# Pooled attention feeding a gated unit: bfloat16 norm broadcasts, a shift that is split before one fp16 transpose, and a lead for the output divisions in a list schedule

## The chip, the cores and the metric

The kernel runs on one core of one Trainium2 chip. The metric is the device time of one execution in microseconds (us); the median of several runs is compared. The core's engines are named as the profile names them: PE is TensorE (PEld is its weight load, which overlaps the multiplying), DVE is VectorE, ACT is ScalarE, POOL is GpSimd and SP is SyncE, which here issues all DMAs.

## What is computed

The reference has two stages. The first is attention for 8 batches of 8 heads, with 1152 keys of 64 elements and queries averaged in pairs to 576; the second is a gated feed-forward unit whose gate mixes the positions of the sequence.

```python
q_pool = q.reshape(B, H, S // 2, 2, D).mean(axis=3)
scores = np.matmul(q_pool, k.transpose(0, 1, 3, 2)) / np.sqrt(D)
scores = scores - np.max(scores, axis=-1, keepdims=True)
attn = np.exp(scores)
attn = attn / (np.sum(attn, axis=-1, keepdims=True) + 1e-09)
x = np.matmul(attn, v)                       # heads side by side: 8 x 576 x 512
h = np.maximum(x @ w_in, 0.0)
u, g = h[..., :512], h[..., 512:]
g_n = (g - mean(g)) / np.sqrt(var(g) + 1e-06)
g_s = np.einsum('ts,bsd->btd', w_spatial, g_n) + b_spatial[None, :, None]
out = (u * g_s) @ w_out
```

Everything is float32 for the caller. Inside, each float32 operand is held as a sum of two 16-bit parts (a head and a rest), and products are made of 16-bit matmuls.

## The kernel before

**Units of attention.** Two heads of one batch make a unit; there are 32 units. Unit i needs, ahead of its own loop, `prep(i)` (the queries and keys scaled and split into fp16 parts), `maxima(i)` (the maximum of the scores of each query, from a cheaper product of the fp16 heads alone) and `shift` (the maxima turned into two extra rows of the matmul operand X, so that the product already comes out shifted). `attention(i)` then makes, for each of the two heads, nine tiles of 128 keys by 512 queries: two matmuls into PSUM (L796, L797), the exponential on ACT (L802, into a buffer `pt`, of which there are 8), and on POOL the subtraction that leaves the rest of the tile as fp16 (L822). The last 64 queries of both heads go through tail tiles (L809, L813, L818). `values(i, k)` multiplies a finished tile with the values: twelve short matmuls (L714, L720, L725) that add up over the nine tiles of a head in one PSUM tile `o`. There is one buffer for `o`. When the ninth tile is in, the sums are divided by the denominators: `inverse` makes `den` (L693 and L694), and L733 writes the quotient `xm`. Only then may the next head's first L714 write `o`; and a `pt` buffer is free again only when its L725 has run.

**The maxima.** For each of 9 blocks of 128 queries, three matmuls of 384 columns (L617, and L608 for the block of tails) go to PSUM tiles `pm` or `pw`, and a DVE reduction (L623, `mt`) takes the maximum of each. After block 5 and after block 9, `shift` runs: it reduces `mt` to `mx` with one column for each block (L635, 128 partitions by 5 or 4 columns), PE transposes `mx` in float32 into a `pm` tile of 5 or 4 partitions by 128 columns (L639), and DVE subtracts and scales it there (L642), casts it to fp16 (L645) and subtracts the cast for the rest (L646). Two DMAs put the two rows into X (L649).

**Norms.** `scales` gets a sum of squares per partition, adds it up over the partitions and broadcasts it with one float32 matmul against a tile of ones (L345), and three small DVE operations (L350, L355, L356) make powers of two of it. It runs once for each unit (`sq`, two columns), and for the values of each batch (`vt`), the gate (`gt`) and the three weights (one column each).

**The gated unit.** Two batches (8 units) at a time, `gated_unit` makes the second stage: products with w_in (L879, L943), the spatial mixing (L984, L985) and w_out (L1027). Its steps are taken between those of the attention of later units. Until the first 8 units are done there is none of this work; in that time the weights are loaded and converted from doubles by large DVE and ACT operations (L384 to L396).

**The order of the work.** The program is first written in the order in which the generators are stepped. Then `Order.pin` puts each engine's instructions into a new order with a list schedule: it goes through modelled time with costs from `cost`, and on each engine takes, of the instructions that are ready at the modelled time, the one that stands first in the program. That order is then fixed with dependencies. A lock is modelled as well: `two_from_sbuf` names DVE operations whose inputs all lie in SBUF, and `pin` lets such an operation and one of POOL not overlap. The engines execute in that order, each instruction waiting for what it depends on.

Of the kernel before, what the change touches and what calls it, by code (L numbers as in the profile page):

```python
# [10 lines left out]
F16 = mybir.dt.float16  # L11
# [20 lines left out]
class Order:  # L32
# [6 lines left out]
    def __init__(self):  # L39
        self.slot = {}  # L40
        self.count = {}
        self.lined = []
        self.seen = 0

# [12 lines left out]
    def line(self, tc, skip=False):  # L57


        n = len(tc.nc.cur_bb.bb.instructions)  # L60
        self.lined.append((self.seen, n, skip))
        self.seen = n

# [119 lines left out]
    def pin(self, tc):  # L183
# [29 lines left out]
        load = {n for n, i in enumerate(prog) if lane[n] == "SP" and i.ins and i.ins[0].bass_ap.tensor.name not in self.slot}  # L213
        last = {}
        dep = mybir.DependencyInfo(mybir.DependencyClass.NoSync, mybir.DependencyReason.DATA)
        for _ in prog:
            best = None
            for e, ns in ready.items():
                if ns:

                    at = {n: max(due[n], wire - 1000) if n in load else due[n] for n in ns}
                    t = max(free[e], min(at.values()))
                    n = min(n for n in ns if at[n] <= t)
                    if best is None or t < best[0]:
                        best = (t, e, n)
# [36 lines left out]
def attn_sgu_kernel(ctx: ExitStack, tc: tile.TileContext, qT, kT, v, w_in, w_spT, b_sp, w_out, out):  # L262
# [41 lines left out]
    ones = const.tile([P, P], F32, name="ones")  # L304
    nc.vector.memset(ones, 1.0)

# [33 lines left out]
    def scales(sq, name, up=0):  # L340
# [4 lines left out]
        nc.tensor.matmul(pt[:, :n], lhsT=ones, rhs=sq, start=True, stop=True)  # L345
# [285 lines left out]
    def shift(st, mt, a, z):  # L631
# [7 lines left out]
        nc.tensor.transpose(out=pt[:n, :P], in_=mx[:, :n], identity=ident)  # L639
        mr = sm.tile([NT, 2, P], F16, name="mr", bufs=2)  # L640
        m = pt[:n, :P]
        nc.vector.tensor_scalar(  # L642
            out=m, in0=m, scalar1=st["lnp"][:n], scalar2=1.0 / MROW, op0=ALU.subtract, op1=ALU.mult
        )
        nc.vector.tensor_copy(out=mr[:n, 0], in_=m)  # L645
        nc.vector.tensor_sub(mr[:n, 1], m, mr[:n, 0])  # L646
        for r in range(2):
            rows = X[D + r : D + r + 1].rearrange("p h s -> p (h s)")
            nc.sync.dma_start(out=rows[:, a * P : z * P], in_=mr[:n, r])  # L649
# [7 lines left out]
    LAG = 2  # L657
    TAIL_SPLIT = 5
# [41 lines left out]
    def values(i, k):  # L700
# [28 lines left out]
        if c == NC - 1:  # L729
            if h == 0:  # L730
                st["xm"] = wk.tile([P, 4, P], F32, name="xm")
            r = inverse(o[:, :, D], "den")
            nc.vector.tensor_tensor(  # L733
                out=st["xm"][:, :, h * D : (h + 1) * D], in0=o[:, :, 0:D],
                in1=r.unsqueeze(2).to_broadcast([P, 4, D]), op=ALU.mult,
            )
# [450 lines left out]
```

## Time and profile before

| | us |
|---|---|
| median of three runs | 1226.53 (1224.41 to 1229.68) |
| span of the profiled execution | 1225.3 |
| PE busy | 1153.0 (94%) |
| DVE busy | 906.2 (74%) |
| ACT busy | 889.2 (73%) |
| POOL busy | 875.8 (71%) |

The profile is of one execution, whose span of 1225.3 us from the first to the last instruction is its own time; the median of the runs is 1.2 us above it. A row of instructions gives the busy time in all, the mean of one in ns, and the idle time of the engine ahead of it with what ended that idle time. A row of the timeline gives the start, the time it took, the engine and line, and in brackets the idle time before it. Matmuls are pipelined: the record of one lasts longer than the time by which it holds up the next, so what a matmul costs PE is read from one start to the next. Consecutive short DVE records overlap as well.

In 40 slices, PE is below 90% busy up to about 280 us and at 90% or more in nearly all slices after that; the granted clock is 0.8 to 0.9 in parts of the first 280 us and full afterwards.

### The profile page before, as it was taken

To read this page: it belongs to the slowest core of one execution; us is meant where nothing else is said; L and a number is where in the kernel's file an instruction comes from. 1 tells how busy PE (TensorE), PEld (TensorE's weight loads), DVE (VectorE), ACT (ScalarE), POOL (GpSimd) and SP (SyncE) were. 2 spreads that over 40 slices of the span, in tenths; PEclk is the share of its full clock that TensorE was granted. 3 is DMA by queue.
4 is the path that set the end of the run, shared out by engine and by line. 5 is a ranking of instruction groups with operands and counts; after the bars stand their busy time and mean duration, and the time that the engine had idled before them with its cause. 6 is when DMAs were issued, how large, how long until landed. Compare 5 with 4: busy or idle time off the path is not lost.

```text
span 1225.3 us, 34090 instructions
## 1 busy us (share of the span) xinstructions
PE 1153.0 (94%) x13632; PEld 725.7 (59%) x13632; DVE 906.2 (74%) x2187; ACT 889.2 (73%) x1659; POOL 875.8 (71%) x750
## 2 busy tenths in 40 slices
PE   3878888889999999999999999999999999999998
PEld 1545566556666666666666666566666666665453
DVE  5699999977889678766679686865669867851644
ACT  4788669778977877868777787878777876754433
POOL 2769979898887877777788877778887776764000
PEclk9899999999999999999999999999999999999999
DMA  5454454446333443155322442146422321111002
GB/s 188 157 180 133 118 180 123 110 115 173 113 89 94 133 126 101 51 145 170 93 75 75 132 134 74 53 133 198 113 75 75 90 84 43 30 45 36 1 1 78
DMA packets 62335, 126.70 MB, mean 103 GB/s; under 512 B 13728, under 2 KB 21920, under 8 KB 61664
## 3 DMA queue, kind: packets, MB, share of 16 engines
q1 hardware_dynamic: 62176, 124.52, 34.7%
q8 instruction: 107, 1.75, 0.6%
q14 instruction: 52, 0.43, 0.1%
HBM read 81.20 MB, written 9.44 MB: 74 GB/s over the span
## 4 chain that ended last, share of the span: by engine, by line
PE 72%; DVE 8%; ACT 2%; POOL 1%; issue 1%; DMA 1%; SPq 1%; ACTq 0%; DVEq 0%; POOLq 0%
PE pss L797 7%; PE pss L796 7%; PE pm L617 7%; PE pw L984 6%; PE pw L879 6%; PE pw L1027 6%; PE pw L943 5%; PE o L725 4%; PE o L714 4%; PE o L720 4%; DVE mt L623 3%; DVE vv L372 2%; PE pss L879 1%; PE pss L984 1%; PE pss L1027 1%
## 5 line engine op out<-in xcount | busy, mean ns | idle before, releaser
L822 POOL TENSOR_TENSOR pt<-pt 128x512 f16<-128x512 f32 x576 | 641.6, 1134 | 185.3 <-ACT pt L802 183.3
L802 ACT ACTIVATE pt<-pss,esc 128x512 f32<-128x512 f32 x576 | 387.7, 687 | 150.0 <-PE pss L797 114.3
L623 DVE TENSOR_REDUCE mt<-pm 128x1 f32<-128x384 f32 x733 | 387.1, 548 | 70.7 <-PE pm L617 61.9
L796 PE MATMUL pss<-qhi,khi 128*128 128x512 f16 x576 | 220.5, 384 | 13.9 <-ACT pt L802 12.8
L797 PE MATMUL pss<-xq,klo 66*128 66x512 f16 x576 | 221.1, 385 | 1.3 <-DMA xq<-mr 1.3
L617 PE MATMUL pm<-khi,qhi 128*128 128x384 f16 x655 | 205.5, 330 | 10.9 <-DVE mt L623 5.9
L714 PEld LDWEIGHTS <-pt 128*128 128x128 bf16 x2304 | 132.2, 99 | 69.1 <-issue 4.7
L725 PE MATMUL o<-vp,pt 128*128 128x65 f16 x2304 | 169.6, 194 | 2.5 <-POOL pt L822 2.4
L714 PE MATMUL o<-vp,pt 128*128 128x65 f16 x2304 | 170.8, 194 | 0.2
L720 PE MATMUL o<-vp,pt 128*128 128x64 f16 x2304 | 168.3, 194 | 0.0
L725 PEld LDWEIGHTS <-pt 128*128 128x128 f16 x2304 | 121.1, 99 | 26.9 <-POOL pt L822 5.0
L617 PEld LDWEIGHTS <-qhi 128*128 128x128 f16 x768 | 73.8, 99 | 81.9 <-issue 38.0
L720 PEld LDWEIGHTS <-pt 128*128 128x128 bf16 x2304 | 112.3, 99 | 3.3 <-issue 0.5
L879 PE MATMUL pw<-wi_h,xg 128*128 128x512 f16 x240 | 88.7, 378 | 0.2 <-DVE mt L623 0.2
L818 ACT ACTIVATE ptl<-pss,esc 128x256 f32<-128x256 f32 (+1 forms) x128 | 63.9, 499 | 27.8 <-PE pss L813 27.0
L822 POOL TENSOR_TENSOR ptl<-ptl 128x1152 f16<-128x1152 f32 x32 | 70.3, 2197 | 18.8 <-ACT ptl L818 18.8
L1027 PE MATMUL pw<-wo_h,vv 128*128 128x512 f16 x216 | 79.7, 379 | 3.9 <-DVE vv L372 3.9
L797 PEld LDWEIGHTS <-klo 66*128 66x128 f16 x576 | 57.1, 99 | 43.3 <-issue 17.4
L984 PE MATMUL pw<-ws_h,vv 128*128 128x512 f16 x216 | 80.6, 379 | 0.0
L943 PE MATMUL pw<-xg,wi_h 128*128 128x512 f16 (+1 forms) x336 | 80.6, 325 | 0.0
L623 DVE TENSOR_REDUCE mt<-pw 128x1 f32<-128x384 f32 x131 | 69.2, 541 | 11.1 <-PE pw L617 10.7
L796 PEld LDWEIGHTS <-khi 128*128 128x128 f16 x576 | 56.7, 99 | 21.0 <-issue 3.6
(194 smaller groups left out, 2446.1 us busy)
## 6 DMA issues: line engine op xcount, KB each, us to landing
vt<-in_v_dram SPq DMA_DIRECT2D x56, 576.0 KB
qt<-in_qT_dram SPq DMA_DIRECT2D x32, 576.0 KB
kt<-in_kT_dram SPq DMA_DIRECT2D x32, 576.0 KB
khi<-kn SPq DMA_DIRECT2D x128, 144.0 KB
out_dram<-row SPq DMA_DIRECT2D x24, 256.0 KB
qhi<-xq SPq DMA_DIRECT2D x64, 72.0 KB
klo<-klo SPq DMA_DIRECT2D x32, 144.0 KB
vv<-in_w_in_dram SPq DMA_DIRECT2D x4, 1024.0 KB
```

The source lines that it names most:

```text
L617: nc.tensor.matmul(pm[:, :W], lhsT=qhl[:, h, c0 : c0 + P], rhs=khh[:, h, n * NB : (n + 1) * NB, :], start=True, stop=True,)
L623: nc.vector.reduce_max(out=mt[:, t, n : n + 1], in_=pm[:, :W], axis=AX.X)
L714: nc.tensor.matmul(o[:, t], lhsT=top[:, cols], rhs=vp[:, D : D + D1], start=c == 0 and t == 0, stop=False, skip_group_check=True,)
L720: nc.tensor.matmul(o[:, t, 0:D], lhsT=top[:, cols], rhs=vp[:, 0:D], start=False, stop=False, skip_group_check=True)
L725: nc.tensor.matmul(o[:, t], lhsT=rst[:, cols], rhs=vp[:, D : D + D1], start=False, stop=c == NC - 1, skip_group_check=True,)
L796: nc.tensor.matmul(o, lhsT=khh[:, h, c, :], rhs=qhl[:, h, q], start=True, stop=False)
L797: nc.tensor.matmul(o, lhsT=KL[0:KR, h, c, :], rhs=X[0:KR, h, q], start=False, stop=True)
L802: nc.scalar.activation(pt, ps, AF.Exp, bias=0.0, scale=esc)
L822: nc.gpsimd.tensor_sub(t.bitcast(F16)[..., 0::2], t, t.bitcast(BF16)[..., 1::2])
L879: nc.tensor.matmul(ph, lhsT=xa[:, cc, c0 : c0 + P], rhs=wa[:, cc, DH:DF], start=n == 0, stop=n == 3 * NCC - 1,)
L984: nc.tensor.matmul(pv, lhsT=l, rhs=r[:, 0:MAIN], **fl)
L1027: nc.tensor.matmul(py, lhsT=ga[:, fc, c0 : c0 + P], rhs=wa[:, fc, :], start=m == 0, stop=m == end - 1)
```

## The change

Three things are changed; the products, tiles and buffers stay.

1. **Norms.** The tile of ones is bfloat16, and the matmul in `scales` takes the upper halves of the float32 sums as bfloat16. The profile before shows two matmul records for each float32 product; a bfloat16 product is one matmul with one weight load.
2. **Shift.** The subtraction, the scaling and the split into two fp16 parts are made on the columns of `mx` in SBUF, 128 partitions by 5 or 4 columns, ahead of the transpose. Both parts stand side by side in `mc` and are transposed by one fp16 transpose into 10 or 8 partitions of a PSUM tile, and one copy brings them to `mr`. The two DMAs are the same.
3. **Lead.** The instructions of the division (the two of `inverse` and the product) are written inside `order.sooner`, which notes a lead of 400 places for each. `pin` chooses among the ready instructions of an engine by place in the program less lead.

```diff
+    def sooner(self, tc, steps, make):
+        ins = tc.nc.cur_bb.bb.instructions
+        n = len(ins)
+        make()
+        for i in tc.nc.cur_bb.bb.instructions[n:]:
+            self.lead[i.name] = steps
...
+        rank = [n - self.lead.get(i.name, 0) for n, i in enumerate(prog)]
...
-                    n = min(n for n in ns if at[n] <= t)
+                    n = min((n for n in ns if at[n] <= t), key=rank.__getitem__)
...
-    ones = const.tile([P, P], F32, name="ones")
+    ones = const.tile([P, P], BF16, name="ones")
     nc.vector.memset(ones, 1.0)
+    ident_h = const.tile([P, P], F16, name="ident_h")
+    nc.vector.tensor_copy(out=ident_h, in_=ident)
...
-        nc.tensor.matmul(pt[:, :n], lhsT=ones, rhs=sq, start=True, stop=True)
+        nc.tensor.matmul(pt[:, :n], lhsT=ones, rhs=sq.bitcast(BF16)[:, 1::2], start=True, stop=True)
...
-        nc.vector.reduce_max(out=mx[:, :n], in_=mt[:, a:z], axis=AX.X)
-        yield
-        yield
-        pt = ps_m.tile([P, 512], F32, name="pm")
-        nc.tensor.transpose(out=pt[:n, :P], in_=mx[:, :n], identity=ident)
-        mr = sm.tile([NT, 2, P], F16, name="mr", bufs=2)
-        m = pt[:n, :P]
-        nc.vector.tensor_scalar(
-            out=m, in0=m, scalar1=st["lnp"][:n], scalar2=1.0 / MROW, op0=ALU.subtract, op1=ALU.mult
-        )
-        nc.vector.tensor_copy(out=mr[:n, 0], in_=m)
-        nc.vector.tensor_sub(mr[:n, 1], m, mr[:n, 0])
+        m = mx[:, :n]
+        nc.vector.reduce_max(out=m, in_=mt[:, a:z], axis=AX.X)
+        nc.vector.tensor_scalar(out=m, in0=m, scalar1=st["lnp"], scalar2=1.0 / MROW, op0=ALU.subtract, op1=ALU.mult)
+        mc = sm.tile([P, 2, NT], F16, name="mc", bufs=2)
+        mh, ml = (mc.rearrange("p r t -> p (r t)")[:, r * n : (r + 1) * n] for r in range(2))
+        nc.vector.tensor_copy(out=mh, in_=m)
+        nc.vector.tensor_sub(ml, m, mh)
+        yield
+        yield
+        pt = ps_m.tile([P, 512], F32, name="pm").bitcast(F16)[: 2 * n, :P]
+        nc.tensor.transpose(out=pt, in_=mc.rearrange("p r t -> p (r t)")[:, : 2 * n], identity=ident_h)
+        mr = sm.tile([2 * NT, P], F16, name="mr", bufs=2)
+        nc.vector.tensor_copy(out=mr[: 2 * n], in_=pt)
...
+    LEAD = 400
...
-            r = inverse(o[:, :, D], "den")
-            nc.vector.tensor_tensor(
+            def divide():
+                r = inverse(o[:, :, D], "den")
+                nc.vector.tensor_tensor(
...
+            order.sooner(tc, LEAD, divide)
```

The order of the instructions moves on every engine. Two places are shown. The first is DVE at the seventh division of the program (the first head of the fourth unit), where the second unit after it is being prepared. Names: `mx` and `mr` belong to the shift, `mt` to the maxima, `qhi` and `klo` to `prep`, `vv` to the conversion of a weight, `vr` and `vs` to a norm. Before:

```order
L372 SCALAR_TENSOR_TENSOR qhi_119<-qt,qks,xq_113 128x576
L645 CAST mr<-pm 5x128
L350 TENSOR_SCALAR pm<-pm 128x1
L390 TENSOR_SCALAR vv<-vv 128x1024
L646 TENSOR_TENSOR mr<-pm,mr 5x128
L355 TENSOR_SCALAR vr<-pm 128x1
L356 TENSOR_SCALAR vs<-pm 128x1
L623 TENSOR_REDUCE mt<-pw 128x1
L623 TENSOR_REDUCE mt<-pm 128x1 x2
L372 SCALAR_TENSOR_TENSOR klo_107<-kt,qks,kn 128x640
L623 TENSOR_REDUCE mt<-pm 128x1
L693 TENSOR_SCALAR den<-o 128x4
```

The same place in the changed program, from the row in which the unit's `mx` is reduced (before, that row stands four rows above the first one shown, 15 rows ahead of the division; here it stands three ahead):

```order
L648 TENSOR_REDUCE mx<-mt 128x5
L635 TENSOR_REDUCE mt<-pw 128x1
L568 TENSOR_SCALAR lnp<-lnp 128x1
L707 TENSOR_SCALAR den<-o 128x4
L649 TENSOR_SCALAR mx<-mx,lnp 128x5
L708 RECIPROCAL den<-den 128x4
L384 SCALAR_TENSOR_TENSOR qhi_121<-qt,qks,xq_115 128x576
L749 TENSOR_TENSOR xm<-o,den 128x4x64
L652 CAST mc<-mx 128x5
L635 TENSOR_REDUCE mt<-pw 128x1
L653 TENSOR_TENSOR mc<-mx,mc 128x5
L402 TENSOR_SCALAR vv<-vv 128x1024
```

The division has moved ahead of the rows of `prep`, of the weight and of the maxima that stood before it, and the three steps of the shift now read and write `mx` and `mc` in SBUF, where they read `pm` in PSUM.

The second place is PE at the end of the same head, where `o` changes hands. Before, the last product of the head and the first four rows behind it:

```order
L725 LDWEIGHTS pt
L725 MATMUL o<-vp_100,pt 128x65
L796 LDWEIGHTS khi_114
L796 MATMUL pss<-qhi_117,khi_114 128x512
L797 LDWEIGHTS klo_105
L797 MATMUL pss<-xq_111,klo_105 128x512
```

In the changed program, the last product of that head and all that stands up to the first product of the next:

```order
L629 LDWEIGHTS qhi_120
L629 MATMUL pw<-khi_117,qhi_120 128x384
L739 LDWEIGHTS pt
L739 MATMUL o<-vp_102,pt 128x65
L814 LDWEIGHTS khi_117
L814 MATMUL pss<-qhi_120,khi_117 128x512
L728 LDWEIGHTS pt
L728 MATMUL o<-vp_102,pt 128x65
```

Before, 99 rows (exponent tiles, eleven matmuls of the maxima and the tail's products) stand between the last product of this head and the first of the next; now it is two.

More of the change, by code (lines that the diff above doesn't have):

```diff
@@ L43, in __init__ @@
         self.seen = 0
+        self.lead = {}
     def pool(self, pool, bufs, psum=False):
@@ L731, in values @@
                 st["xm"] = wk.tile([P, 4, P], F32, name="xm")
-            r = inverse(o[:, :, D], "den")
[L733 to L736, printed above, removed]
+            def divide():
+                r = inverse(o[:, :, D], "den")
+                nc.vector.tensor_tensor(
+                    out=st["xm"][:, :, h * D : (h + 1) * D], in0=o[:, :, 0:D],
+                    in1=r.unsqueeze(2).to_broadcast([P, 4, D]), op=ALU.mult,
+                )
+            order.sooner(tc, LEAD, divide)
             if h == 1:
```

2 lines of the change are left out of this document (1 added, 1 removed).

## The prediction

> **What bounds the kernel now.** I first cut the span into stretches. The columns are the length and the busy us (with instructions) of PE, PEld, DVE, ACT and POOL, then the granted clock and the DMA share.
>
> ```profile
> 40.00:280.00 240.00, 201.57 (x2666) 133.57 (x2663) 214.05 (x479) 186.38 (x340) 204.37 (x159) 0.94 0.49 147
> 280.00:1120.00 840.00, 830.67 (x10219) 532.26 (x10215) 616.46 (x1531) 643.70 (x1205) 658.08 (x571) 1.00 0.35 99
> ```
>
> Two regimes. From 280 us on PE is busy for 830.67 of 840 us, and no other engine is near that: there only PE's own work counts. From 40 to 280 us no engine is full. DVE is the fullest, 214.05 of 240, idle for 26; PE is idle for 38.
>
> Next the waits in that first stretch, as "who <- for whom: us in total, times, longest". First ACT's:
>
> ```profile
> ACT pt L802 <- PE o L725: 18.7, 8, 5.3
> ```
>
> The exponentials wait 18.7 us for a `pt` buffer, and a buffer comes free when its products with the values have run. The timeline says why these are late. The head whose sums are the seventh to be divided ends on PE here, and the next begins:
>
> ```profile
> 146.73 0.28 PE L725 MATMUL o<-vp,pt 128*128 128x65 f16 x4
> ...
> 159.81 0.28 PE L714 MATMUL o<-vp,pt 128*128 128x65 f16 x4
> ```
>
> DVE in between (start, length):
>
> ```profile
> 148.87 0.34 DVE L642 TENSOR_SCALAR pm<-pm,lnp 5x128 f32<-5x128 f32 x1
> 149.51 1.43 DVE L372 SCALAR_TENSOR_TENSOR qhi<-qt,qks,xq 128x576 f16<-128x576 f32 x1 [0.31 <-POOL pt L822]
> 150.87 0.27 DVE L645 CAST mr<-pm 5x128 f16<-5x128 f32 x1
> 151.06 0.14 DVE L350 TENSOR_SCALAR pm<-pm 128x1 int32<-128x1 int32 x1
> 151.13 1.26 DVE L390 TENSOR_SCALAR vv<-vv 128x1024 int32<-128x1024 int32 x1
> 152.31 0.27 DVE L646 TENSOR_TENSOR mr<-pm,mr 5x128 f16<-5x128 f32 x1
> 152.51 0.14 DVE L355 TENSOR_SCALAR vr<-pm 128x1 int32<-128x1 int32 x1
> ...
> 159.34 0.42 DVE L733 TENSOR_TENSOR xm<-o,den 128x256 f32<-128x256 f32 x1
> ```
>
> and ACT:
>
> ```profile
> 160.43 0.69 ACT L802 ACTIVATE pt<-pss,esc 128x512 f32<-128x512 f32 x1 [4.12 <-PE o L725]
> ```
>
> The sums are complete at 147.0 (146.73 plus 0.28), the last step of the division runs from 159.34 to 159.76; the next product follows 0.05 us later and ACT, idle for 4.12 us, right behind. So in this stretch the single `o` buffer waits about 12 us in DVE's queue, and ACT stands behind it. PE is then held back by ACT, and DVE in turn by PE. DVE's waits from 40 to 280 us:
>
> ```profile
> DVE mt L623 <- PE pw L617: 6.4, 5, 4.3
> DVE pm L642 <- PE pm L639: 6.0, 4, 3.1
> DVE dent L693 <- PE pm L770: 5.5, 4, 2.3
> DVE pm L350 <- PE pm L345: 3.1, 1, 3.1
> ```
>
> 21.0 of DVE's 26 idle us are waits for a late PE.
>
> **The change part by part: PE after 280 us.** The matmuls that shrink cost, from start to start:
>
> ```profile
> 969.78 0.27 PE L639 MATMUL pm<-ident,mx 128*5 128x128 f32 x1
> 969.89 0.28 PE L345 MATMUL pm<-vt,ones 128*128 128x1 f32 x2
> 970.03 0.38 PE L943 MATMUL pw<-xg,wi_h 128*128 128x512 f16 x1
> ```
>
> A float32 transpose holds PE for 0.11 us, a float32 norm (two matmuls) for 0.14 behind a wide matmul. Behind a short one it is more, as here:
>
> ```profile
> 649.79 0.28 PE L714 MATMUL o<-vp,pt 128*128 128x65 f16 x4
> 649.91 0.36 PE L345 MATMUL pm<-sq,ones 128*128 128x2 f32 x2
> 650.13 0.28 PE L720 MATMUL o<-vp,pt 128*128 128x64 f16 x4
> ```
>
> 0.22 us. The nearest 16-bit rows: four matmuls of 65 columns take 0.12 (649.79 to 649.91), 0.03 each; and for one of 128 columns:
>
> ```profile
> 619.42 0.22 PE L769 MATMUL pm<-vp,ptl 128*128 128x128 f16 x1
> 619.47 0.22 PE L770 MATMUL pm<-vp,ptl 128*128 128x130 f16 x1
> ```
>
> 0.05. The counts after 280 us:
>
> ```profile
> L345 PE MATMUL pm<-sq,ones x44: 165/250/251, 296.6 to 1035.0; 128*128 128x2 f32 x44
> L345 PE MATMUL pm<-vt,ones x10: 168/210/250, 405.7 to 969.9; 128*128 128x1 f32 x10
> L345 PE MATMUL pm<-gt,ones x10: 167/250/250, 492.1 to 1201.1; 128*128 128x1 f32 x10
> ```
>
> ```profile
> L639 PE MATMUL pm<-ident,mx x47: 269/272/276, 280.5 to 1088.7; 128*4 128x128 f32 x24, 128*5 128x128 f32 x23
> ```
>
> 64 records are 32 norms, each saving 0.11 to 0.19; I take 0.13, since most stand behind wide matmuls: 4.2 us. 47 transposes save 0.055: 2.6. Sum 6.8 us, all on the engine that sets the pace; bounds 4 (the bfloat16 weights not hidden) to 9. The trace shows a step of 0.11 under a record of 0.27, so narrowing the moving rows shortens the step. The Trainium skill, "TensorE: Matmul & The Clock Gate", section "Part 4: PE-mode transpose", gives about 275 ns for a transpose that is 16-bit already, as long as the float32 record here; by that figure the transposes would gain nothing and the sum would be 4.2. It is a length, and the trace's steps decide.
>
> **DVE, the shift.** Up to 280 us there are 15:
>
> ```profile
> L639 PE MATMUL pm<-ident,mx x15: 270/272/276, 61.5 to 267.4; 128*5 128x128 f32 x8, 128*4 128x128 f32 x7
> ```
>
> Gone from each: the scaling (about 0.27 once the overlap of records is taken off its 0.34), the cast (150.87 to 151.06, 0.19) and the difference (152.31 to 152.51, 0.20): 0.66. Added: three operations on 5 or 4 columns, whose nearest row is L350 with a step of 0.07 (151.06 to 151.13), and a copy of the transposed rows, priced as the cast: 3 × 0.07 + 0.19 = 0.40. That is 0.26 less for each shift. But the three new operations have all operands in SBUF, where the removed ones had PSUM. DVE operations of that kind show two prices in the trace:
>
> ```profile
> L915 DVE TENSOR_SCALAR row<-vv,mv,rs 128x512 f32<-128x512 f32 x36 | 28.5, 802 | 0.2
> ```
>
> ```profile
> L915 DVE TENSOR_SCALAR row<-vv,mv,rs x36: 509/548/1486, 355.6 to 1163.3; 128x512 f32<-128x512 f32 x36
> ```
>
> Alone 509 ns, on average 802: 0.29 us more. A small operation that never shows it:
>
> ```profile
> L556 DVE TENSOR_SCALAR lnp<-lnp x32: 131/144/155, 9.7 to 1036.5; 128x1 f32<-128x1 f32 x32
> ```
>
> Bounds for the wait of each: 0 (L556, one column) to about 0.65 (the copies under the rivals). I take 0.29, because L915 is the same operation: 0.87 for the three, net +0.61 for each shift, +9 us of DVE work up to 280 us. Afterwards 47 × 0.61 = 29 us fall into DVE's 224 idle us (840 less 616.46): nothing, as long as that cover holds.
>
> **The lead.** In the new order the division stands right behind its sums, and PE has one exponent tile's matmul between the heads. What waits instead is what was queued ahead of the division: reductions of the maxima, `prep` and weight conversions, each later by at most the division's own time. The 18.7 us of ACT go for the most part, and with them PE's and DVE's waits. But DVE has the same work as before, so what can be won is bounded by its waits: 0 to 21.0 us. I take three quarters, 16, since one in four may come from elsewhere (loads, POOL). After 280 us PE hides the division, so the lead is worth nothing there.
>
> Up to 280 us: −16 + 9 = −7; PE's savings there hide behind DVE. The new `ident_h`, the DMAs of the shift and SP's new order are costed at nothing: the loads are issued about two units ahead, and the copy of identity is one small operation at the start.
>
> **Sum.** 1225.3 − 6.8 − 7 = 1211.5 us of span. The median of the runs stands 1.2 us above the profiled span, so I predict 1213.
>
> **Rivals.**
> A (forecast): as above; with its bounds 1206 to 1220. Chance 0.50.
>
> B, small operations do not wait for POOL: L556 speaks for it. The shift then gives 15 × 0.26 = 4 us: 1225.3 − 6.8 − 16 − 4 = 1198.5, so 1200. Chance 0.18.
>
> C, the lead only reorders: DVE's idle time shrinks by no more than the 9 us that the shift adds, because DVE had a backlog anyway (the division was late since other work was ready). PE's saving alone is left, at its low end 4: 1221, so 1222. For it speaks that DVE is already busy for 89% of the stretch. Chance 0.20.
>
> D, the other side: each new small operation waits for a whole operation of POOL. Rows of copies on DVE beside a busy POOL (minimum/median/maximum ns; the minimum is from the end of the program, where POOL is idle):
>
> ```profile
> L924 DVE COPY te<-vv x4: 279/868/918, 376.3 to 1159.4; 64x512 f16<-64x512 f16 x4
> ```
>
> ```profile
> L926 DVE COPY te<-vv x4: 290/998/1034, 380.5 to 1160.0; 64x512 f16<-64x512 f16 x4
> ```
>
> They wait 0.59 and 0.71 us. With 0.65 for each of three a shift costs 1.95 − 0.26 = 1.7 us more: +25 up to 280 us, of which perhaps 10 fall into idle time: +15. After 280 us, stretches with the gated unit's normalising have no cover left:
>
> ```profile
> 640.00:680.00 40.00, 39.91 (x491) 25.68 (x490) 37.35 (x77) 30.04 (x56) 29.51 (x25) 1.00 0.26 73
> ```
>
> DVE has 2.65 us free there and would get two shifts, 3.4; with three such stretches and the displaced reductions I count +4. 1225.3 + 15 + 4 − 6.8 = 1237.5, so 1239. It decides from the point where 15 shifts cost more than the lead gives back and PE saves (16 + 6.8 = 22.8, so 1.5 us each). The Trainium skill, "SBUF — State Buffer", section "Who interferes with whom", speaks for D: casts, copies and scalings between SBUF operands, and any operation with two SBUF inputs, share a port with GpSimd, and the later one waits for the other's whole instruction. By that rule this is what the change does; L915 and L926 agree for 512 columns, and no row shows it for 4 or 5. Chance 0.12.
>
> **How the numbers follow.** About 0.5% (6 us) is what a measurement of this kernel can tell from no change. Faster than 1220.4: A, but for its upper edge, and B, 0.63. Within 0.5% (1220.4 to 1232.7): C and the edges of A and D, 0.25. Slower: D, 0.12. The range that holds 8 in 10 leaves out the lower half of B and most of D: 1200 to 1228. The forecast's own range is 1206 to 1220.
>
> **What would show it.** In the profile after: L345's successor with one matmul record and a step near 0.03; the transposes with a step near 0.055; PE's stretch after 280 us shorter by about 7 us. The wait of ACT for the products in the first stretch well under 18.7 us, and the division within 2 us of its sums. The three small DVE operations of the shift at 0.15 us when alone, about 0.4 on average; near 0.15 always would be B, near 0.8 D. DVE's waits for PE still near 21 us with the division early would be C. It would be wrong as a whole if PE showed new waits after 280 us, since then the new order costs what the matmuls save.

## The result and the profile after

The changed kernel takes 1254.49 us (median of 4 runs, 1250.26 to 1255.11) where the kernel before takes 1225.47 us (median of 4, 1223.69 to 1229.68): a ratio of 1.0224, 95% interval 1.0203 to 1.0245. It is 29 us slower. The forecast was 1213 us, faster than before, with a range of 1206 to 1220 and of 1200 to 1228 for 8 in 10; rival D had 1239. The profiled execution has a span of 1252.3 us against 1225.3, so 27.0 us are to be found.

The stretches of the changed kernel, with the columns of the prediction's first table:

```profile
40.00:280.00 240.00, 195.62 (x2485) 128.27 (x2484) 217.10 (x445) 170.17 (x309) 186.96 (x146) 0.88 0.45 136
280.00:1120.00 840.00, 823.17 (x9994) 517.12 (x9994) 694.51 (x1620) 646.64 (x1211) 648.24 (x567) 1.00 0.35 100
```

In the first stretch DVE is as busy as before (217.10 us, before 214.05), but it gets through 445 instructions instead of 479, and PE, ACT and POOL get through fewer as well. So less of the program is done by 280 us. The granted clock of the stretch is 0.88, where it was 0.94; what that adds to the time is not separated here, but it does not order the losses (e5 below is further behind with 0.91). Afterwards DVE has 78 us more to do (694.51 against 616.46), and PE is busy for 7.5 us less of the same 840 us.

How far behind the program is can be read from the sixteenth division (in both kernels the sixteenth record of `xm<-o,den`). Before:

```profile
290.83 0.42 DVE L733 TENSOR_TENSOR xm<-o,den 128x256 f32<-128x256 f32 x1
```

After:

```profile
308.69 0.41 DVE L749 TENSOR_TENSOR xm<-o,den 128x256 f32<-128x256 f32 x1
```

17.9 of the 27.0 us are lost by then, in the part that was forecast to win 7. The other 9.1 are lost behind it, where 6.8 were to be won. Such a reading is of one execution each: two executions of the same program differ at this point by 3.6 and 3.7 us (e3 and e12, e2 and e11 below).

What DVE does longer is in the groups by shape, here from 40 to 280 us (busy us, mean ns of one, idle us before them): the three steps of the shift that now work on `mx` and `mc` in SBUF.

```profile
L652 DVE CAST mc<-mx 128x4 f16<-128x4 f32 x7 | 5.8, 836 | 0.0
L653 DVE TENSOR_TENSOR mc<-mx,mc 128x4 f16<-128x4 f32 x7 | 4.9, 695 | 0.0
L653 DVE TENSOR_TENSOR mc<-mx,mc 128x5 f16<-128x5 f32 x7 | 4.4, 624 | 0.0
L649 DVE TENSOR_SCALAR mx<-mx,lnp 128x4 f32<-128x4 f32 x7 | 4.3, 613 | 0.0
L649 DVE TENSOR_SCALAR mx<-mx,lnp 128x5 f32<-128x5 f32 x7 | 4.2, 607 | 0.0
L652 DVE CAST mc<-mx 128x5 f16<-128x5 f32 x7 | 4.2, 593 | 0.0
```

42 operations on four or five columns take 27.8 us, 0.66 each. The shortest records of the three lines in the whole run are 218, 156 and 138 ns, 0.17 us on average, so each waits for about 0.49 us in this stretch. Three of them make 1.47 us for a shift, where the prediction had 0.87.

The seventh division, the one that the prediction followed, now reads so (the rows of PE and DVE that bear on it):

```profile
160.25 0.19 PE L739 MATMUL o<-vp,pt 128*128 128x65 f16 x1
...
160.47 0.16 DVE L707 TENSOR_SCALAR den<-o 128x4 f32<-128x4 f32 x1 [0.20 <-PE o L739]
160.55 1.06 DVE L649 TENSOR_SCALAR mx<-mx,lnp 128x5 f32<-128x5 f32 x1
...
161.53 0.16 DVE L708 RECIPROCAL den<-den 128x4 f32<-128x4 f32 x1
161.61 1.58 DVE L384 SCALAR_TENSOR_TENSOR qhi<-qt,qks,xq 128x576 f16<-128x576 f32 x1
...
163.12 0.41 DVE L749 TENSOR_TENSOR xm<-o,den 128x256 f32<-128x256 f32 x1
...
163.59 0.18 PEld L728 LDWEIGHTS <-pt 128*128 128x128 bf16 x4 [3.24 <-DVE xm L749]
```

The lead does what it says: DVE takes up `den` as soon as the sums are complete (160.25 plus 0.19), and the division has ended 3.1 us after them, where it took 12.8. Inside those 3.1 us stands one of the new small operations, with 1.06 us for five columns, in front of the reciprocal. ACT's waits in the first stretch ("who <- for whom: us in total, times, longest") follow:

```profile
ACT pt L820 <- PE pss L815: 28.8, 25, 6.2
...
ACT pt L820 <- PE o L739: 9.3, 5, 4.2
```

The wait for the products with the values has halved, from 18.7 to 9.3 us. But ACT now waits for 28.8 us for PE's products of scores, where the row of before (`L802 <- PE pss L797`) had 7.2. PE waits itself in the meantime. The longest of its waits for DVE is now the one for the shift's split, which the change put ahead of the transpose and for which the prediction has no term. Before, the weight load of the transpose waited for `mx`:

```profile
PEld pm L639 <- DVE mx L635: 2.0, 5, 0.6
```

After, for `mc`:

```profile
PEld L657 <- DVE mc L653: 13.9, 8, 4.6
```

And DVE's waits for PE after:

```profile
DVE dent L707 <- PE pm L788: 6.1, 5, 2.3
DVE mr L659 <- PE pm L657: 5.3, 6, 3.1
DVE den L707 <- PE o L739: 3.1, 5, 1.3
DVE mt L635 <- PE pm L629: 2.8, 11, 0.4
DVE mt L635 <- PE pw L629: 2.5, 1, 2.5
DVE pm L362 <- PE pm L357: 2.0, 2, 1.7
```

Together 21.8 us, as against 23.4 for all six rows of before (the prediction shows the four longest, 21.0). That is the sign that the prediction named for rival C: the division early, and DVE's waits where they were.

On PE the 16-bit norm keeps its promise and the 16-bit transpose does not. Before, a float32 transpose behind a short matmul:

```profile
613.60 0.29 PE L725 MATMUL o<-vp,pt 128*128 128x65 f16 x4
...
613.73 0.27 PE L639 MATMUL pm<-ident,mx 128*5 128x128 f32 x1
...
613.83 0.38 PE L796 MATMUL pss<-qhi,khi 128*128 128x512 f16 x1
```

After, the fp16 transpose behind a short matmul, and a bfloat16 norm:

```profile
655.91 0.19 PE L739 MATMUL o<-vp,pt 128*128 128x65 f16 x1
656.03 0.22 PE L657 MATMUL pm<-ident_h,mc 128*8 128x128 f16 x1
656.18 0.27 PE L739 MATMUL o<-vp,pt 128*128 128x65 f16 x3
...
712.16 0.17 PE L357 MATMUL pm<-sq,ones 128*128 128x2 bf16 x1
712.18 0.22 PE L961 MATMUL pw<-xg,wi_l 128*128 128x128 f16 x1
```

The norm's step is 0.02 to 0.03 us (0.14 before). The transpose's step is 0.15 (0.11 before; forecast 0.055), and the matmul ahead of it waits to be followed as well: its own step is 0.12, where the last of the four before took about 0.03. Over all transposes after 280 us, the time from the start of the last matmul ahead to the start of the one behind, where nothing waits, is 0.137 us before and 0.274 after (0.272 to 0.276, once 0.248) behind a short matmul, and 0.324 and 0.46 behind one of 512 columns. That is 0.137 us more for each, 6.4 us for 47, where 2.6 less was forecast.

### The profile page after: what moved, and what is told of

Same layout as the page of the kernel before. It is cut to its first block, busy times and chain, and to the rows that moved or that the text cites. A ratio compares the mean times of both kernels' runs of the same rounds, so it can differ in the third digit from the quotient of the medians.

```text
span 1252.3 us, 33981 instructions
## 1 busy us (share of the span) xinstructions
PE 1165.8 (93%) x13584; PEld 721.3 (58%) x13584; DVE 991.2 (79%) x2252; ACT 891.9 (71%) x1659; POOL 867.6 (69%) x750
## 4 chain that ended last, share of the span: by engine, by line
PE 72%; DVE 15%; ACT 2%; issue 2%; DMA 1%; POOL 1%; SPq 0%; ACTq 0%; DVEq 0%
PE pm L629 8%; PE pss L815 7%; PE pss L814 7%; PE pw L897 6%; PE pw L1045 6%; PE pw L1002 6%; PE pw L961 5%; DVE mt L635 4%; PE o L739 4%; PE o L728 4%; PE o L734 4%; PE pm L786 1%; PE pm L788 1%; PE pm L787 1%; PE pss L897 1%
## 5 line engine op out<-in xcount | busy, mean ns | idle before, releaser
L840 POOL TENSOR_TENSOR pt<-pt 128x512 f16<-128x512 f32 x576 | 632.9, 1117 | 231.4 <-ACT pt L820 228.7
L814 PE MATMUL pss<-qhi,khi 128*128 128x512 f16 x576 | 221.3, 385 | 11.5 <-ACT pt L820 10.6
L629 PE MATMUL pm<-khi,qhi 128*128 128x384 f16 x655 | 211.7, 336 | 6.3 <-DVE mt L635 2.9
L728 PE MATMUL o<-vp,pt 128*128 128x65 f16 x2304 | 174.5, 195 | 3.7 <-DVE xm L749 2.6
L728 PEld LDWEIGHTS <-pt 128*128 128x128 bf16 x2304 | 133.0, 99 | 76.8 <-DVE xm L749 10.2
L739 PE MATMUL o<-vp,pt 128*128 128x65 f16 x2304 | 173.4, 195 | 0.1
L734 PE MATMUL o<-vp,pt 128*128 128x64 f16 x2304 | 173.2, 195 | 0.0
L739 PEld LDWEIGHTS <-pt 128*128 128x128 f16 x2304 | 128.3, 99 | 47.0 <-issue 10.2
L734 PEld LDWEIGHTS <-pt 128*128 128x128 bf16 x2304 | 114.4, 99 | 5.4 <-issue 2.3
```

The source lines that it names most:

```text
L629: nc.tensor.matmul(pm[:, :W], lhsT=qhl[:, h, c0 : c0 + P], rhs=khh[:, h, n * NB : (n + 1) * NB, :], start=True, stop=True,)
L728: nc.tensor.matmul(o[:, t], lhsT=top[:, cols], rhs=vp[:, D : D + D1], start=c == 0 and t == 0, stop=False, skip_group_check=True,)
L734: nc.tensor.matmul(o[:, t, 0:D], lhsT=top[:, cols], rhs=vp[:, 0:D], start=False, stop=False, skip_group_check=True)
L739: nc.tensor.matmul(o[:, t], lhsT=rst[:, cols], rhs=vp[:, D : D + D1], start=False, stop=c == NC - 1, skip_group_check=True,)
L814: nc.tensor.matmul(o, lhsT=khh[:, h, c, :], rhs=qhl[:, h, q], start=True, stop=False)
L840: nc.gpsimd.tensor_sub(t.bitcast(F16)[..., 0::2], t, t.bitcast(BF16)[..., 1::2])
```

## The experiments

**Theory P** (rival D's mechanism): DVE operations with their operands in SBUF wait for POOL's whole operations even when they are four columns wide; this is the loss. **Rivals**: the lead's order costs the time; the matmuls' new forms cost it; or it is only the added work and the order, not the port. Medians of before beside the runs were 1225.1 to 1226.1 us throughout.

### The three parts alone

Each takes lines of the change's diff into the kernel before. e1, the shift:

```diff
+    ident_h = const.tile([P, P], F16, name="ident_h")
+    nc.vector.tensor_copy(out=ident_h, in_=ident)
...
+        nc.vector.tensor_scalar(out=m, in0=m, scalar1=st["lnp"], scalar2=1.0 / MROW, op0=ALU.subtract, op1=ALU.mult)
...
+        nc.tensor.transpose(out=pt, in_=mc.rearrange("p r t -> p (r t)")[:, : 2 * n], identity=ident_h)
...
```

e2, the lead:

```diff
+    LEAD = 400
...
+            order.sooner(tc, LEAD, divide)
```

e3, the norms, and e4, which is e3 and e2 together:

```diff
+    ones = const.tile([P, P], BF16, name="ones")
...
+        nc.tensor.matmul(pt[:, :n], lhsT=ones, rhs=sq.bitcast(BF16)[:, 1::2], start=True, stop=True)
```

> The kernel before with the new shift alone. Theory P (each of the three small SBUF operations waits for an operation of POOL, 0.56 us on average, and DVE's extra work stretches the first 300 us): 1245 to 1260, and the three operations at 0.6 to 0.8 us each as in the changed kernel. Theory L (the lead is what costs, since it pushes the maxima back on a full DVE): 1222 to 1232, although the operations show the same waits.

> The kernel before with the lead alone. Theory P: no loss, 1210 to 1226, ACT's wait for products with the values well under 18.7 us. Theory L: 1240 to 1255, the first stretch longer by some 20 us.

> The kernel before with the bfloat16 norms alone. Both theories: 32 norms after 280 us save 0.13 us each, 4 us: 1219 to 1224, unless the new order of the list schedule by itself moves the time, which would show here as a change of more than 4 us either way with the first stretch changed.

> The change without the new shift: norms and lead. Theory P: the loss is gone and the norms' 4 us are there, 1205 to 1222. Theory L: still slower than before, 1236 to 1252.

| | median us | ratio to before, 95% interval |
|---|---|---|
| e1 shift | 1257.55 | 1.0271 [1.0245, 1.0297] |
| e2 lead | 1237.23 | 1.0091 [1.0058, 1.0123] |
| e3 norms | 1225.68 | 1.0008 [0.9982, 1.0034] |
| e4 norms and lead | 1230.19 | 1.0052 [1.0033, 1.0072] |

The shift alone costs more than the whole change. The norms bring nothing that can be measured, although their matmuls shrink as forecast. And the lead, with the old shift, costs time: 4.5 us from e3 to e4, and 11.7 alone. e1 is as theory P expected; e2 and e4 lie between the times of the two theories.

In e2 one DVE operation stands out. The rows of DVE and POOL around it:

```profile
296.50 12.01 DVE L382 SCALAR_TENSOR_TENSOR qhi<-qt,qks,xq 128x576 f16<-128x576 f32 x1
...
299.02 1.24 POOL L536 TENSOR_TENSOR vp<-vt,vp 128x576 f16<-128x576 f32 x1
...
300.22 1.40 POOL L591 TENSOR_TENSOR klo<-kt,kn 128x640 f16<-128x640 f32 x1
...
301.57 3.04 POOL L837 TENSOR_TENSOR pt<-pt 128x512 f16<-128x512 f32 x3
...
304.57 1.23 POOL L536 TENSOR_TENSOR vp<-vt,vp 128x576 f16<-128x576 f32 x1
...
305.75 1.15 POOL L591 TENSOR_TENSOR klo<-kt,kn 128x512 f16<-128x512 f32 x1
...
306.86 1.04 POOL L837 TENSOR_TENSOR pt<-pt 128x512 f16<-128x512 f32 x1
```

An operation of 0.8 us, with two inputs in SBUF, takes 12.01 us. It ends at 308.51, 0.61 us after POOL has nothing left to do (306.86 plus 1.04); the eight POOL operations shown, and two ahead of them, start one behind the other during its record. From 300 to 310 us PE is busy for 1.03 of 10 us. Repeats of e2 and e3 asked whether this belongs to the order:

> The lead alone once more, to see whether the 12.01-us DVE operation (the qhi split at 296.5 us) belongs to the order or to one execution. If it belongs to the order: again one DVE operation with two SBUF inputs of 8 us or more near 296 us, time 1232 to 1240. If to the execution: the longest DVE operation in the stretch from 280 to 320 us is under 4 us, span lower by 5 to 10 us, 1227 to 1233.

> The norms alone once more, for the same question on the 8.45-us operation at 281.5 us. If it belongs to the order: again one of 6 us or more near 281 us, time 1222 to 1230. If to the execution: none over 4 us there, and the norms' saving of about 5 us shows, 1218 to 1222.

e11 (the lead) took 1243.09 us in its one run, above the expected range, and the row of the same line (shortest, median, longest ns) is:

```profile
L382 DVE SCALAR_TENSOR_TENSOR qhi<-qt,qks,xq x32: 796/830/12583, 10.4 to 1055.2; 128x576 f16<-128x576 f32 x32
```

So with that order it comes again. The norms, which have the like at another place, differ. e3:

```profile
L372 DVE SCALAR_TENSOR_TENSOR wo_l<-u,wos,wo_h x2: 2054/5252/8449, 281.5 to 289.9; 128x1024 f16<-128x1024 f32 x2
```

e12, the same program:

```profile
L372 DVE SCALAR_TENSOR_TENSOR wo_l<-u,wos,wo_h x2: 1262/1264/1267, 281.8 to 283.0; 128x1024 f16<-128x1024 f32 x2
```

There it belongs to the execution. But without it e12 still took 1225.1 us (span 1223.3), not the 1218 to 1222 expected: the norms' 5 us are mostly not in the time even so, and the long wait does not explain that.

### Is it the port?

e5 adds three dead operations to each shift of before, on `mx` in SBUF (their results go nowhere); e9 adds the first of them alone:

```diff
         nc.vector.reduce_max(out=mx[:, :n], in_=mt[:, a:z], axis=AX.X)
+        dm = sm.tile([P, NT], F32, name="dm", bufs=2)
+        nc.vector.tensor_scalar(out=dm[:, :n], in0=mx[:, :n], scalar1=1.0, scalar2=None, op0=ALU.add)
+        for _ in range(2):
+            nc.vector.tensor_scalar(out=dm[:, :n], in0=dm[:, :n], scalar1=1.0, scalar2=None, op0=ALU.add)
```

e6 adds three reciprocals of the same size instead, a kind that shows no wait in the profile after (L708 took 0.16 us above):

```diff
+        nc.vector.reciprocal(dm[:, :n], mx[:, :n])
+        for _ in range(2):
+            nc.vector.reciprocal(dm[:, :n], dm[:, :n])
```

> The kernel before, with three more operations in each shift whose result nothing reads: tensor_scalar on the 5 or 4 columns of mx, SBUF to SBUF. Theory P (such operations wait for POOL's): 0.6 to 0.8 us each on average, 1.7 us more for each shift, 1245 to 1260, as far as the new shift alone. Theory R (not the wait but the longer chain of the shift and the new order cost): the result hangs on nothing, so 1224 to 1235.

> The same with three reciprocals on the same columns in place of the tensor_scalars; reciprocals of 4 columns in SBUF never took over 180 ns in the kernel before. Theory P: no waits, three steps of 0.07 to 0.1 us, 1225 to 1233. Theory R: the same as with the tensor_scalars, within 5 us.

> The kernel before with one dead tensor_scalar (SBUF to SBUF, 4 or 5 columns) in each shift instead of three. Theory P (each such operation waits by itself for GpSimd, and DVE's idle time in the first stretch cannot take it up): a third of what three cost (+39.7 us), so +10 to +16 us, 1236 to 1241, with the operation's mean record near 0.7 us. Rival Q (it is the chain of three dependent operations that costs, or DVE's idle time takes up the first of them): +0 to +5 us, 1225 to 1230.

e5 took 1265.17 us (1.0317 [1.0271, 1.0363]; above the 1245 to 1260 expected), e6 1226.44 (1.0002 [0.998, 1.0024]), e9 1236.89 (1.0095 [1.0064, 1.0126]). One group of each with 5 columns; e5:

```profile
L639 DVE TENSOR_SCALAR dm<-dm 128x5 f32<-128x5 f32 x64 | 49.7, 777 | 0.2
```

e6:

```profile
L637 DVE RECIPROCAL dm<-mx 128x5 f32<-128x5 f32 x32 | 5.9, 185 | 0.5
```

e9:

```profile
L637 DVE TENSOR_SCALAR dm<-mx 128x5 f32<-128x5 f32 x32 | 21.5, 671 | 0.5
```

As many operations of the same size on the same engine cost 39 us as scalings and nothing as reciprocals. One scaling costs 10.8 us, somewhat over a quarter of three. In e5's trace the waits of the added operations up to the sixteenth division (each record less the shortest of its kind) sum to 22.7 us, and the program is 25.8 us behind there (316.61 against 290.83): DVE's idle time took up none of it. e5 loses another 10.1 us behind that point although nothing reads these results, and PE waits there for late maxima (`PE pm L617 <- DVE mt L623` 6.4 us, before 0.5). The planner models the lock too and knows the scalings as SBUF operations but not the reciprocals, so the orders of e5 and e6 differ as well; the durations of 777 and 185 ns do not come from an order, but how much of the 39 us does is not separated.

e7 is the whole change with `mx` in the PSUM tile that the transpose uses anyway, so that each of the three small operations has an input in PSUM; e8 is e7 with `LEAD = 0`.

```diff
-        mx = sm.tile([P, NT], F32, name="mx", bufs=2)
-        m = mx[:, :n]
+        ps = ps_m.tile([P, 512], F32, name="pm")
+        m = ps[:, 256 : 256 + n]
...
-        pt = ps_m.tile([P, 512], F32, name="pm").bitcast(F16)[: 2 * n, :P]
+        pt = ps.bitcast(F16)[: 2 * n, :P]
```

> The whole change, but mx lies in the PSUM tile that the transpose then writes: the scaling and the cast read PSUM, the difference has one SBUF input. The chain and its length are the same. Theory P: the three operations at 0.15 to 0.2 us, 1218 to 1234 (the norms' and transposes' saving less what the lead costs). Theory R: 1245 to 1256, as the change itself.

> The same with the lead at 0. If the lead costs 5 us or more also here, this is faster than with the lead by that much and than the kernel before: 1212 to 1224. If the lead's cost was a matter of one order alone: within 4 us of the run with the lead.

e7 took 1226.51 us (0.9996 [0.9972, 1.0019]) and e8 1230.6 (1.0026 [1.0003, 1.0049]). The three operations in e7:

```profile
L649 DVE TENSOR_SCALAR pm<-pm,lnp 128x5 f32<-128x5 f32 x32 | 7.2, 226 | 0.6
...
L652 DVE CAST mc<-pm 128x5 f16<-128x5 f32 x32 | 5.1, 158 | 0.3
...
L653 DVE TENSOR_TENSOR mc<-pm,mc 128x5 f16<-128x5 f32 x32 | 5.1, 159 | 0.3
```

No wait is left, and 28.0 of the 29.0 us are gone. The list schedule gives e7 another order than the changed kernel, so the 28.0 are not free of that; but the waits are gone from every record, and e5 lost time with waits of the same size and no new chain. Theory P holds. The Trainium skill, "SBUF — State Buffer", section "Who interferes with whom", has the rule (casts and scalings can, and operations with two SBUF inputs do, contend with GpSimd for a shared pair of ports, and the one that comes later is blocked for the other's whole instruction); the traces agree down to four columns, with about half a microsecond of wait on average, but the long waits of e2 and e11 outlast ten and eleven instructions.

But e7 is rival B come true, with 1200 forecast for it, and it stands at 1226.5. Two of the prediction's gains are therefore missing without any port: the lead's 16 us and PE's 6.8. The lead is worth 4.1 us between e8 and e7; with the old shift it costs. That e8 is the slower of the two is what neither of its expectations named.

### Where PE's saving went

e10 is before with e7's shift alone. e13 is before with each float32 transpose made four times into the same tile, to see whether PE's work goes into the time at all.

```diff
-        nc.tensor.transpose(out=pt[:n, :P], in_=mx[:, :n], identity=ident)
+        for _ in range(4):
+            nc.tensor.transpose(out=pt[:n, :P], in_=mx[:, :n], identity=ident)
```

> The shift of the change alone, with mx reduced into and worked on in PSUM; norms and lead as before. Theory P with nothing else behind the shift's price: the small operations stay near 0.15 us, each shift is 0.26 us lighter on DVE and PE saves 2.6 us in its transposes: 1219 to 1225. Rival R (the transposes now stand behind a longer DVE chain on PE, which gives the matmuls' saving back): 1225 to 1229, with PE's weight loads for the transposes waiting for mc over 5 us after 280 us.

> The kernel before with each float32 transpose of the shift made four times instead of once, into the same tile: three more steps of 0.11 us on PE for each of 62 shifts, 15.5 us after 280 us and 5.0 before, DVE's work as it was. If PE sets the pace after 280 us in the strict sense that the prediction used (its work goes into the time one for one): +13 to +20 us, 1239 to 1246. If PE's schedule there has slack that small changes of its work move in and out of (which would also explain why 5 us fewer in the norms bring nothing): +3 to +10 us, 1229 to 1236.

e13 took 1243.75 us (1.0159 [1.0138, 1.018]): 18.2 us for some 21 us of added work (192 transposes, 0.11 us each). In its trace nothing is lost up to the sixteenth division (287.56, before 290.83) and 20.1 us behind it, where some 15 were added (the list schedule's order moved as well). So PE does set the pace after 280 us, and a saving there should show. e10 took 1230.23 us (1.0033 [1.0011, 1.0055]), above both of its expected ranges, though DVE's part of the shift is lighter there. By its trace it is 7.4 us ahead of before at the sixteenth division (283.43) and loses 9.0 us behind it. PE's loads of `mc` wait for DVE there for 6.9 us in 18 waits (before, those of `mx`: 1.4 in 5), as the rival of the expectation has it, which can be a part of the 9.0. That left the transposes themselves. The first guess was the mode of the instruction. e14, e15, e16 and e17 are e7, e10, the changed kernel and e8 with a plain matmul against the same identity:

```diff
-        nc.tensor.transpose(out=pt, in_=mc.rearrange("p r t -> p (r t)")[:, : 2 * n], identity=ident_h)
+        nc.tensor.matmul(out=pt, lhsT=mc.rearrange("p r t -> p (r t)")[:, : 2 * n], rhs=ident_h, start=True, stop=True)
```

> The whole change with mx in PSUM, and the fp16 transposes made as plain matmuls of mc against the fp16 identity (into float32 rows in PSUM) instead of as transposes. Theory T (a 16-bit transpose costs PE 0.274 us from the start of the matmul ahead of it to the start of the one behind, against 0.137 for the float32 one, because nothing overlaps with it; a plain matmul costs 0.03 + 0.055): 0.19 us less for each of 62 shifts, 9 us of it after 280 us, against 1226.5 with the transposes: 1214 to 1219, faster than before. Rival (the transposes' price is a matter of records and hides): 1224 to 1229.

> The shift alone in PSUM (1230.2 with transposes), with plain matmuls instead. Theory T: 9 to 12 us less, 1218 to 1222. Rival: 1228 to 1232.

> The change as it is (mx and mc in SBUF, 1254.5), with plain matmuls instead of transposes and nothing else. Theory T: the part after 280 us, 47 x 0.19 = 9 us, comes off, and in the first stretch little, since DVE paces it there: 1243 to 1248. Rival: 1252 to 1256.

> As e14 with the lead at 0 (1230.6 with transposes). Theory T: 1219 to 1223, and the lead's worth is again e14 against this, 4 us by the pair with transposes. If the lead's worth is a matter of how one order happens to fall, the pair differs by under 2 us or the other way.

They took 1226.64, 1230.42, 1251.78 and 1231.24 us: as with the transposes, but for 2.7 us in e16, whose interval (1.0191 to 1.0236) overlaps that of the changed kernel. e14 and e17 repeat the lead's worth: 4.6 us. Theory T fell, and the traces say why: the plain matmul has the same step, 0.274 us from the matmul ahead to the one behind. What all these share is a 16-bit stationary of 10 or 8 columns, and its weight load shows the oddity. In the changed kernel:

```profile
642.24 0.08 PEld L657 LDWEIGHTS <-mc 128*10 128x10 f16 x1 [0.24 <-DVE stt L907]
642.24 0.22 PE L657 MATMUL pm<-ident_h,mc 128*10 128x128 f16 x1
```

Load and matmul start within 2 ns of each other, and so they do in all 49 after 280 us, while the float32 loads of 5 or 4 columns in before start 28 ns ahead at the median. e18 is e7 with `mc` 128 columns wide, the rest zeros:

```diff
+    mcs = [const.tile([P, P], F16, name=f"mc{i}") for i in range(2)]
+    for t in mcs:
+        nc.vector.memset(t, 0.0)
...
-        mc = sm.tile([P, 2, NT], F16, name="mc", bufs=2)
+        mc = mcs[0]
+        mcs.reverse()
...
-        pt = ps.bitcast(F16)[: 2 * n, :P]
-        nc.tensor.transpose(out=pt, in_=mc.rearrange("p r t -> p (r t)")[:, : 2 * n], identity=ident_h)
+        pt = ps.bitcast(F16)[:, :P]
+        nc.tensor.transpose(out=pt, in_=mc, identity=ident_h)
```

> The whole change with mx in PSUM (1226.5), and the transposes' stationary mc widened from 10 or 8 columns to 128 (the rest zeros, never read on). With the transposes and with plain matmuls alike the 16-bit step over 10 or 8 columns took PE 0.274 us from the start of the matmul ahead to the start of the one behind, its weight load starting with the matmul in every one of 46 records instead of ahead of it. Theory W (16-bit loads of fewer than 128 columns are not overlapped, and that ate the norms' saving): the same distance falls to 0.08 to 0.12 us behind a short matmul, the load starts ahead, and 62 x 0.15 to 0.19 us come off: 1215 to 1220, faster than before. Rival (the step is as long whatever the width, or PE's waits take it back): 1223 to 1229.

e18 took 1221.06 us (median of 10, 1215.13 to 1223.7; 0.9954 [0.9937, 0.9972]): 5.4 us faster than e7, and the one kernel here whose interval lies below before. The time is between the ranges of theory W and of the rival, nearer to W's; the distance is as W said. The end of a short matmul, the transpose and the next product in its timeline:

```profile
627.02 0.29 PE L743 MATMUL o<-vp,pt 128*128 128x65 f16 x4
627.11 0.10 PEld L661 LDWEIGHTS <-mc 128*128 128x128 f16 x1
627.14 0.22 PE L661 MATMUL pm<-ident_h,mc 128*128 128x128 f16 x1
...
627.20 0.38 PE L818 MATMUL pss<-qhi,khi 128*128 128x512 f16 x1
```

The load starts ahead of its matmul again (27 ns at the median), the step is 0.06 us, and from the matmul ahead to the one behind it is now 0.084. All engines run the same rows in the same order in e7 and e18 (but for the two memsets), so nothing else changed. The transposes' 0.19 us over 46 after 280 us make 8.7, of which 5.4 are in the time (4.8 with each kernel set against its own runs of before). No width between 10 and 128 columns was run. Behind the sixteenth division e18 takes 929.4 us, where before took 934.4: 5.0 of the 6.8 us that the prediction wanted from PE there, once the stationary is wide.

## Why the prediction was wrong

A gain of 12 us was forecast, and the kernel lost 29. Three steps of the sum failed. The shift, with the waits of its small operations, was taken to add 9 us up to 280 us and nothing afterwards; it added about 18 there and a part of the 9.1 behind. The lead was taken as 16 us up to 280 us, and none of it shows there. The transposes were to save 2.6 us, and they cost 6.4.

The 29.0 us can be put together from three pairs of kernels: SBUF instead of PSUM for the small operations 28.0 (from e7 to the changed kernel), the narrow 16-bit stationary 5.4 (from e18 to e7), and all the rest of the change −4.4 (1221.06 against 1225.47). Only e18 and e7 have the same order of instructions; in the other pairs the list schedule's order differs too, which alone moved the time by 4 to 5 us where only the lead changed (e8 to e7, e17 to e14). Step by step:

- **The port: the mechanism was named, the size was off, and its cover did not exist.** The prediction took 0.29 us of wait for each small operation (from L915); the first stretch shows 0.49, the dearer rows L924 and L926 were nearer. For a shift that is 1.47 − 0.26 = +1.2 us, not +0.61, and 15 of them make 18, not 9. Rival D, with 0.65, was near the mark for the mechanism. It then let DVE's idle time take up 10 us; e1 is behind by 21.6 us at the sixteenth division (312.44 against 290.83), where the waits in its 18 shifts sum to 21.8 (17 once the 0.26 by which each shift is lighter is taken off), so nothing fell into idle time. After 280 us the prediction counted "nothing, as long as that cover holds". In the changed kernel PE's loads of `mc` wait there for DVE,

```profile
PEld L657 <- DVE mc L653: 11.5, 18, 1.2
```

  11.5 us in 18 waits (before, for `mx`, 1.4 in 5): the shift's last step had come onto PE's path through the transpose that reads it, though DVE is idle for 145 us of that stretch (840 less 694.51). These are the new waits of PE that the prediction named as the sign of being wrong as a whole. They are not the only way to lose time there: e5, where nothing reads the added operations, loses 10.1 us behind the sixteenth division as well. How the 9.1 us of the changed kernel divide between these waits, late maxima and the transposes is not separated.
- **The lead: the division came early as forecast, and the 16 us did not follow.** DVE's waits for PE stayed (21.8 us, before 23.4). The step that failed reads "I take three quarters, 16": it took the waits behind one late buffer for time that comes free. ACT's wait moved to the scores of the next head, and PE, which has to make them, waits itself for `mc`. That this wait is the cause is not shown: e8 has more of it (18.5 us) and is not behind before at the sixteenth division (290.96). Measured, the lead takes off 4.1 and 4.6 us with the new shift in PSUM (e8 to e7, e17 to e14) and adds 4.5 to 11.7 with the old one; with the new shift in SBUF no run changes the lead alone (from e1 to the changed kernel, 3.1 us, the norms change too). And what it takes off does not lie where it was forecast: at the sixteenth division e7 is 1.6 us ahead of e8 and e14 1.1 behind e17, less than two executions of one program differ, and the other 2.8 and 3.6 us lie behind it, where the prediction counted nothing. So C was right about the first stretch. That it can cost by how one order falls is shown for e2, where one long wait recurs in e11; for e4, which has no such wait, the cause stays open.
- **PE after 280 us: that it sets the pace was right (e13), the norms' steps were right, the transposes' were wrong in sign.** The prediction priced an fp16 transpose by matmuls whose stationary has 128 columns (L769). The nearest row in width, the float32 transpose with its 5 columns, was read as a price of the data type. With 8 or 10 columns in 16 bits it cost 0.137 us more than the float32 one, +6.4 instead of −2.6 us. The Trainium skill, "TensorE: Matmul & The Clock Gate", section "Part 4: PE-mode transpose", gives about 275 ns for a 16-bit transpose of 128 by 128 in a kernel; the prediction set it aside as a record's length. The traces do not bear it out for that size: in e18 such a transpose has a record of 0.22 us and a distance of 0.084. That the distance is 0.274 with 8 or 10 columns is a coincidence of numbers, and not due to the mode, since the plain matmul shows it too.
- **The norms** save some 5 us of PE's work (48 of them, 0.11 each), and e3 and e12 show no more than 2 of them in a span. After 280 us PE waits in e12 for DVE's maxima for 8.3 us, before for 5.0; that this is where the rest went is only argued.
- **The chances**: the rivals were drawn as alternatives, but C and D are about different parts and came together. Put together afterwards, their sum by the prediction's own prices, no gain from the lead and D's +25 up to 280 us, would have been 1225.3 + 25 + 4 − 6.8 = 1247.5 us of span; with the transposes' sign put right (+9.0) it is 1256.5, against 1252.3.

## What to carry to other kernels

In this kernel a scaling, cast or subtraction that moved from PSUM to SBUF next to a busy GpSimd was priced by GpSimd's operations, not by its own width: keep one input in PSUM, or use a kind that shows no wait in the trace, and when a trace has only wide rows of the kind, take the dearest of them for the small ones. A transpose or matmul with a narrow 16-bit stationary can cost PE more than the float32 one it replaces; read its price from the start of the matmul ahead to the start of the one behind, and try the full 128 columns. A step that moves ahead of a PE instruction needs a term of its own for PE's wait. Waits around one late buffer are not time to be won until an experiment has made the buffer early.

## What the runs showed of the hardware

- A DVE operation with two SBUF inputs can wait for many GpSimd operations in a row, not for one alone: its record lasted 12.01 and 12.58 us while ten and eleven of them started one behind the other (e2, e11), and 8.45 us while seven did (e3). In the same program it came in one execution and not in another (e3, e12).
- The wait does not shrink with the width: records on four or five columns reach 1.69 us (L652 in the changed kernel), while reciprocals on tiles of that size stay at 0.15 to 0.19 (e6).
- A 16-bit stationary of 8 or 10 columns took 0.274 us of PE between its neighbours behind a short matmul, one of 128 columns 0.084, whether as a transpose (e7, e18) or, for the narrow one, as a plain matmul (e14). The float32 one of 4 or 5 columns took 0.137.
